# Instance normalisation of 32 x 576 planes: a compact gamma/beta load broadcast by TensorE, batched matmuls and merged stores

## Chip, cores, metric

One core of a Trainium2 chip. The metric is the device time of one execution in microseconds (us), median of several; lower is better. Ratios below are the mean time of one kernel's fast runs over that of the kernel before in the same rounds, so they are not quite the ratio of the medians quoted beside them. e1 to e4 ran on one chip, e5 to e8 on a second and e9 to e12 on a third; across chips only ratios are compared closely.

## The reference

```python
B, C, H, W = 32, 576, 16, 32        # x: bf16, g, b: bf16 of length C
mu = x.mean(axis=(-2, -1), keepdims=True)
var = ((x - mu) * (x - mu)).mean(axis=(-2, -1), keepdims=True)
xhat = (x - mu) / jnp.sqrt(var + 1e-5)
return xhat * g.reshape(1, -1, 1, 1) + b.reshape(1, -1, 1, 1)
```

18.87 MB are read and 18.87 MB written.

## The kernel before

All of x fits in SBUF. Each of the 128 partitions holds 144 consecutive planes ("tiles" 0 to 143: one plane of 512 elements per partition). Because 576 = 4 x 144, partition p needs row p mod 4 of gamma and beta seen as a 4 x 144 matrix. Tiles go in batches of two kinds: D takes its statistics on VectorE (`bn_stats`), P takes the mean by matmuls with a scaled identity and the variance by a ScalarE square with accumulation. ScalarE, GpSimd and, at the end, VectorE then apply scale and bias in place. A small scheduler in Python fixes every engine's order when the program is built.

```python
xr   = x.rearrange("b c h w -> (b c) (h w)").rearrange("(p n) f -> p n f", p=P)
g_src = bass.AP(g.tensor, 0, [[0, P // Q], [NT, Q], [1, NT]])     # 128 rows of 144, each row read 32 times
...
# GpSimd, behind its iota: gamma and beta by the software queue
em.eng.dma_start(g_sb[:], g_src).then_inc(sGB, 16)
em.eng.dma_start(b_sb[:], b_src).then_inc(sGB, 16)
...
# sync engine: 20 loads of 2, 2, 4, 8, 8, ... tiles, then one store for each batch or half batch
for ci, (a, e_) in enumerate(load_chunks):
    sp.dma_start(xt[:, a:e_, :], xr[:, a:e_, :]).then_inc(ld_sems[ci], 16)
for s_ in stores:
    dep_waits(em, [("ap", n) for n in range(s_["t0"], s_["t1"])])
    sp.dma_start(outr[:, s_["t0"]:s_["t1"], :], xt[:, s_["t0"]:s_["t1"], :]).then_inc(sST, 16)
...
# mean of a P tile: 8 matmuls of 64 columns, accumulated
for j in range(JB):
    ins = e.matmul(dst, ident[:], xt[:, n, j * NP_:(j + 1) * NP_], start=(j == 0), stop=(j == JB - 1), ...)
```

Of the kernel before, what the change touches and what calls it, by code (L numbers as in the profile page):

```python
# [11 lines left out]
F32 = mybir.dt.float32  # L12
BF16 = mybir.dt.bfloat16
I32 = mybir.dt.int32
# [5 lines left out]
    sq=704.0,  # L20
    mm=300.0,
    ap_A=705.0,
# [7 lines left out]
    lat=130.0,  # L30
    tile_dma=306.0,
    dma_start=1700.0,
    dma_fixed=60.0,
)
# [44 lines left out]

def build_plan(nt, pattern=None, load_chunks=None, cost=None, store_max=8, use_pool=True, use_pe=True):  # L80
    c = dict(COST)
# [34 lines left out]
    arrive = []  # L116
    t = c["dma_start"]
    for ci, (a, b_) in enumerate(load_chunks):
        t += (b_ - a) * c["tile_dma"] + c["dma_fixed"]
        arrive.append(t)  # L120
        for n in range(a, b_):
            tile_chunk[n] = ci

    tasks = {}
# [9 lines left out]
    add(("SQ0",), "A", 1400.0, [("DS",)], -1)  # L134
    add(("I0",), "G", 200.0, [], -1)
    add(("I1",), "V", 100.0, [("I0",)], -1)
    gb_arrive = 3000.0

# [7 lines left out]
    for b in batches:  # L146
        bi = b["idx"]
        w = b["t1"] - b["t0"]
        sm = c["small"] + c["small_per_elem"] * w
        if b["typ"] == "D":  # L150
            for n in range(b["t0"], b["t1"]):
                add(("bn", n), "V", c["bn"], [("ld", tile_chunk[n])], 10, bi)
            last_bn = [("bn", n) for n in range(b["t0"], b["t1"])]
            add(("R1", bi), "V", sm, last_bn, 1, bi)
            add(("R2a", bi), "V", sm, last_bn, 1, bi)
            add(("R2b", bi), "V", sm, last_bn, 1, bi)
            add(("T2", bi), "V", sm, [("R2a", bi), ("R2b", bi)], 1, bi)
            add(("V", bi), "V", sm, [("T2", bi), ("R1", bi)], 1, bi)
            add(("C1", bi), "A", c["sqrt"], [("V", bi)], 0, bi)
            ms_dep = ("R1", bi)  # L160
        else:
            for n in range(b["t0"], b["t1"]):
                deps = [("ld", tile_chunk[n]), ("I1",)]
                if b["pk"] >= psum_banks:
                    deps.append(("Rd", p_batches[b["pk"] - psum_banks]["idx"]))
                add(("mm", n), "T", c["mm"], deps, 10, bi)
            add(("Rd", bi), "V", c["rd_fixed"] + c["rd_per_tile"] * w, [("mm", n) for n in range(b["t0"], b["t1"])], 1, bi)
            add(("Cp", bi), "V", sm, [("Rd", bi)], 2, bi)
            for n in range(b["t0"], b["t1"]):
                deps = [("Rd", bi)]  # L170
                if len(sq_list) >= junk_n:
                    deps.append(("sq", sq_list[-junk_n]))
                tsq = add(("sq", n), "A", c["sq"], deps, 10, bi)
                tsq.idx_sq = len(sq_list)
                sq_list.append(n)
            add(("C1", bi), "A", c["sqrt"], [("sq", n) for n in range(b["t0"], b["t1"])], 0, bi)
            ms_dep = ("Cp", bi)
        add(("C2", bi), "V", sm + 25, [("C1", bi)], 0, bi)
        add(("C3", bi), "V", sm, [("C2", bi), ("gb",)], 0, bi)
        add(("C4", bi), "V", sm, [("C3", bi), ms_dep], 0, bi)  # L180
        add(("C5", bi), "V", sm, [("C4", bi), ("gb",)], 0, bi)
        for n in range(b["t0"], b["t1"]):
            add(("ap", n), None, None, [("C5", bi)], 50, bi)
# [3 lines left out]
    for ci in range(len(load_chunks)):  # L187
        done[("ld", ci)] = arrive[ci] - lat
    done[("gb",)] = gb_arrive - lat

# [33 lines left out]
    def pick(eng, t):  # L224
# [13 lines left out]
        if best is not None and best[1].cls <= 2:  # L238
            return best[1], None
        if eng == "G" and t < 1200.0 and not pending["G"]:  # L240
            return None, 1200.0
        if soon is not None and eng in ("V", "A"):
# [14 lines left out]
    while n_left > 0:  # L257
# [40 lines left out]
        tnow = min(cand)  # L298

    stores = []  # L300
    for b in batches:
        a = b["t0"]
        while a < b["t1"]:
            e = min(b["t1"], a + store_max)
            rdy = max(tasks[("ap", n)].end for n in range(a, e))
            stores.append(dict(t0=a, t1=e, ready=rdy))
            a = e
    stores.sort(key=lambda s: (s["ready"], s["t0"]))
    tq = arrive[-1]
    for s in stores:  # L310
        tq = max(tq, s["ready"] + 600.0) + (s["t1"] - s["t0"]) * c["tile_dma"] + c["dma_fixed"]
    makespan = max(tk.end for tk in tasks.values())
    return dict(
        nt=nt, batches=batches, load_chunks=load_chunks, stores=stores, tasks=tasks, streams=streams,
        tile_batch=tile_batch, tile_chunk=tile_chunk, makespan=makespan, est_total=tq + 2000.0,
        junk_n=junk_n, psum_banks=psum_banks, cost=c, use_pool=use_pool,
    )


def plan_summary(plan):  # L320
    lines = []
    st = plan["streams"]
    for e in ("V", "A", "G", "T"):
        busy = sum(t.dur for t in st[e])
        end = max([t.end for t in st[e]] or [0])
        kinds = {}
        for t in st[e]:
            kinds[t.key[0]] = kinds.get(t.key[0], 0) + 1
        lines.append(f"  {e}: n={len(st[e])} busy={busy/1e3:.1f}us end={end/1e3:.1f}us {kinds}")
    lines.append(f"  compute makespan {plan['makespan']/1e3:.1f}us  est total {plan['est_total']/1e3:.1f}us")  # L330
    return "\n".join(lines)

# [18 lines left out]
def bass_standalone__instancenorm__sampling_kernel(  # L351
# [29 lines left out]
    outr = out.rearrange("b c h w -> (b c) (h w)").rearrange("(p n) f -> p n f", p=P)  # L381
    g_src = bass.AP(g.tensor, 0, [[0, P // Q], [NT, Q], [1, NT]])
    b_src = bass.AP(b.tensor, 0, [[0, P // Q], [NT, Q], [1, NT]])

    with nc.Block() as block, contextlib.ExitStack() as es:  # L385
# [7 lines left out]
        junk = sb("junk", [P, junk_n, F], BF16)  # L393
        g_sb = sb("g_sb", [P, NT], BF16)
        b_sb = sb("b_sb", [P, NT], BF16)
        st = sb("st", [P, NT, 6], F32)
# [15 lines left out]
        d_ps = ps[:, 4, 2 * NT:3 * NT]  # L412
        rstd_ps = ps[:, 5, 0:NT]
        t_ps = ps[:, 5, NT:2 * NT]
        nm_ps = ps[:, 5, 2 * NT:3 * NT]

# [3 lines left out]
        def dep_waits(em, deps):  # L420
            need = {}
            for d in deps:
                if d[0] == "ld":
                    sem, val = ld_sems[d[1]], 16
                elif d[0] == "gb":
                    sem, val = sGB, 32
                else:
                    pt = tasks[d]
                    sem, val = sem_of[pt.eng], pt.idx + 1
# [15 lines left out]
        def emit_task(em, tk):  # L445
# [7 lines left out]
            elif k == "I0":  # L453
                ins = e.iota(iota_t[:], [[1, P]], base=0, channel_multiplier=-1)
            elif k == "SQ0":
                ins = e.activation(dummy[:, 1:2], dummy[:, 0:1], ACTF.Sqrt)  # L456
# [30 lines left out]
            elif k == "C2":  # L487
                t0, t1 = rng(tk.key[1])
                ins = e.reciprocal(rstd_ps[:, t0:t1], std_sb[:, t0:t1])  # L489
            elif k == "C3":  # L490
                t0, t1 = rng(tk.key[1])
                ins = e.tensor_tensor(scale_sb[:, t0:t1], g_sb[:, t0:t1], rstd_ps[:, t0:t1], ALU.mult)  # L492
            elif k == "C4":
                bb = batches[tk.key[1]]
                t0, t1 = bb["t0"], bb["t1"]
                if bb["typ"] == "D":
                    ins = e.scalar_tensor_tensor(t_ps[:, t0:t1], MA_ps[:, t0:t1, 0], -0.5, scale_sb[:, t0:t1], ALU.mult, ALU.mult)  # L497
                else:
                    ins = e.tensor_tensor(t_ps[:, t0:t1], nm_ps[:, t0:t1], scale_sb[:, t0:t1], ALU.mult)  # L499
            elif k == "C5":  # L500
                t0, t1 = rng(tk.key[1])
                ins = e.tensor_tensor(bias_sb[:, t0:t1], t_ps[:, t0:t1], b_sb[:, t0:t1], ALU.add)  # L502
            elif k == "sq":
# [4 lines left out]
            elif k == "mm":  # L508
                n = tk.key[1]
                bb = batches[tk.batch]  # L510
                slot = n - bb["t0"]
                dst = ps[:, bb["bank"], slot * NP_:(slot + 1) * NP_]
                ins = None
                for j in range(JB):
                    ins = e.matmul(dst, ident[:], xt[:, n, j * NP_:(j + 1) * NP_], start=(j == 0), stop=(j == JB - 1),  # L515
                                   skip_group_check=True)
# [14 lines left out]
        def run_stream(em, name):  # L531
            for tk in streams[name]:
                emit_task(em, tk)
                if name == "G" and tk.key[0] == "I0":
                    em.eng.dma_start(g_sb[:], g_src).then_inc(sGB, 16)
                    em.eng.dma_start(b_sb[:], b_src).then_inc(sGB, 16)

        @block.sync
        def _(sp):
            em = _Emit(sp, None, "SP")  # L540
            for ci, (a, e_) in enumerate(load_chunks):
                sp.dma_start(xt[:, a:e_, :], xr[:, a:e_, :]).then_inc(ld_sems[ci], 16)  # L542
            for s_ in stores:
# [49 lines left out]
```

## Time and profile before

| | before |
|---|---|
| median of the first 4 runs | 98.59 us (97.93 to 98.83) |
| span in the profile | 97.0 us |
| bytes over the span | 391 GB/s; 424 where the pipe is full |
| VectorE, ScalarE, GpSimd busy | 79%, 78%, 71% |
| stores | 24, of 2 to 8 tiles |
| matmuls | 400 of 64 columns |

Loads and stores run one after the other through one queue over sixteen DMA engines. The question for any change is what it does to that pipe: when it starts, when it has holes, and when the last of the sixteen engines finishes. The prediction shows the lines.

### The profile page before, as it was taken

To read this page: it belongs to the slowest core of one execution; us is meant where nothing else is said; L and a number is where in the kernel's file an instruction comes from. 1 tells how busy PE (TensorE), PEld (TensorE's weight loads), DVE (VectorE), ACT (ScalarE), POOL (GpSimd) and SP (SyncE) were. 2 spreads that over 40 slices of the span, in tenths; PEclk is the share of its full clock that TensorE was granted. 3 is DMA by queue.
4 is the path that set the end of the run, shared out by engine and by line. 5 is a ranking of instruction groups with operands and counts; after the bars stand their busy time and mean duration, and the time that the engine had idled before them with its cause. 6 is when DMAs were issued, how large, how long until landed. Compare 5 with 4: busy or idle time off the path is not lost.

```text
span 97.0 us, 1412 instructions
## 1 busy us (share of the span) xinstructions
PE 30.5 (31%) x400; PEld 27.6 (29%) x400; DVE 76.5 (79%) x244; ACT 75.3 (78%) x171; POOL 69.3 (71%) x97
## 2 busy tenths in 40 slices
PE   0220179259489189179767100000000000000000
PEld 0210169149388089079566000000000000000000
DVE  1532748899799899899799999999999999976000
ACT  6061627695599799999999999999999999996000
POOL 6000600498699599999999999999999996991000
DMA  1989999999999999999999999999999999999971
GB/s 40 298 205 379 429 432 422 432 422 399 419 426 426 429 422 405 412 432 422 420 405 409 431 429 430 425 423 411 422 432 429 429 414 438 421 411 426 423 290 58
DMA packets 6407, 37.91 MB, mean 391 GB/s; under 512 B 736, under 2 KB 736, under 8 KB 2944
## 3 DMA queue, kind: packets, MB, share of 16 engines
q1 hardware_dynamic: 6336, 37.75, 94.5%
q0 software_dynamic: 64, 0.07, 0.8%
q8 instruction: 3, 0.05, 0.2%
q14 instruction: 4, 0.03, 0.1%
HBM read 18.95 MB, written 18.87 MB: 390 GB/s over the span
## 4 chain that ended last, share of the span: by engine, by line
ACT 31%; DMA 29%; SPq 13%; DVE 10%; PE 5%; issue 2%; ACTq 1%
DMA xt<-in_x_dram 29%; ACT xt L520 20%; SPq L542 13%; ACT junk L506 11%; DVE st L459 8%; PE ps L515 5%; ACT std_sb L486 1%; ACTq L385 1%; DVE nm_sb L480 1%; DVE ps L489 0%; DVE ps L497 0%; DVE bias_sb L502 0%; DVE scale_sb L492 0%; DVE ps L462 0%; DVE ps L468 0%
## 5 line engine op out<-in xcount | busy, mean ns | idle before, releaser
L523 POOL TENSOR_SCALAR xt<-xt,scale_sb,bias_sb 128x512 bf16<-128x512 bf16 x90 | 67.6, 767 | 17.5 <-DVE bias_sb L502 8.8
L459 DVE BATCH_NORM_STATS2 st<-xt 128x6 f32<-128x512 bf16 x94 | 59.7, 678 | 5.4 <-DMA xt<-in_x_dram 5.4
L506 ACT ACTIVATE junk<-xt,nm_sb 128x512 bf16<-128x512 bf16 x50 | 35.4, 708 | 8.6 <-DVE nm_sb L480 8.6
L520 ACT ACTIVATE xt<-xt,bias_sb,scale_sb 128x512 bf16<-128x512 bf16 x50 | 36.6, 798 | 3.2 <-DVE bias_sb L502 3.2
L515 PE MATMUL ps<-xt,ident 128*128 128x64 bf16 x400 | 30.5, 276 | 23.2 <-DMA xt<-in_x_dram 23.0
L515 PEld LDWEIGHTS ps<-xt,ident 128*128 128x128 bf16 x400 | 27.6, 136 | 25.7 <-DMA xt<-in_x_dram 25.7
L506 ACT ACTIVATION_READ_ACCUMULATOR junk<-xt,nm_sb 128x1 f32 x50 | 9.4, 187 | 0.0
L480 DVE TENSOR_REDUCE nm_sb<-ps 128x8 f32<-128x512 f32 (+3 forms) x9 | 4.7, 525 | 4.3 <-PE ps L515 4.3
L486 ACT ACTIVATE std_sb<-v_sb 128x8 f32<-128x8 f32 (+6 forms) x19 | 3.7, 197 | 1.2 <-DVE v_sb L474 1.1
L489 DVE RECIPROCAL ps<-std_sb 128x8 f32<-128x8 f32 (+6 forms) x19 | 3.7, 198 | 0.8 <-ACT std_sb L486 0.7
L502 DVE TENSOR_TENSOR bias_sb<-ps,b_sb 128x8 f32<-128x8 f32 (+6 forms) x19 | 2.9, 158 | 0.2
L492 DVE TENSOR_TENSOR scale_sb<-g_sb,ps 128x8 f32<-128x8 bf16 (+6 forms) x19 | 2.8, 153 | 0.2
L523 DVE TENSOR_SCALAR xt<-xt,scale_sb,bias_sb 128x512 bf16<-128x512 bf16 x4 | 2.0, 553 | 0.0
L462 DVE TENSOR_REDUCE ps<-st 128x28 f32<-128x56 f32 (+4 forms) x10 | 1.9, 192 | 0.1
L456 ACT ACT_TABLE_LOAD x1 | 1.3, 1283 | 0.7 <-PEq L578 0.7
L497 DVE SCALAR_TENSOR_TENSOR ps<-ps,scale_sb 128x14 f32<-128x14 f32 (+4 forms) x10 | 1.7, 168 | 0.1
L468 DVE TENSOR_REDUCE ps<-st 128x14 f32<-128x28 f32 (+4 forms) x10 | 1.8, 177 | 0.0
L465 DVE TENSOR_REDUCE d_sb<-st 128x14 f32<-128x28 f32 (+4 forms) x10 | 1.7, 166 | 0.0
L471 DVE SCALAR_TENSOR_TENSOR q_sb<-d_sb,ps 128x14 f32<-128x14 f32 (+4 forms) x10 | 1.5, 154 | 0.0
L474 DVE TENSOR_TENSOR v_sb<-q_sb,ps 128x14 f32<-128x14 f32 (+4 forms) x10 | 1.5, 153 | 0.0
L483 DVE COPY ps<-nm_sb 128x8 f32<-128x8 f32 (+3 forms) x9 | 1.5, 162 | 0.0
L499 DVE TENSOR_TENSOR ps<-ps,scale_sb 128x8 f32<-128x8 f32 (+3 forms) x9 | 1.4, 159 | 0.1
(10 smaller groups left out, 2.4 us busy)
## 6 DMA issues: line engine op xcount, KB each, us to landing
xt<-in_x_dram SPq DMA_DIRECT2D x17, 1024.0 KB, 24.1
out_dram<-xt SPq DMA_DIRECT2D x10, 1024.0 KB, 10.3
out_dram<-xt SPq DMA_DIRECT2D x6, 768.0 KB, 8.2
out_dram<-xt SPq DMA_DIRECT2D x2, 640.0 KB, 14.4
out_dram<-xt SPq DMA_DIRECT2D x2, 512.0 KB, 14.4
out_dram<-xt SPq DMA_DIRECT2D x2, 384.0 KB, 14.1
xt<-in_x_dram SPq DMA_DIRECT2D x2, 256.0 KB, 2.9
xt<-in_x_dram SPq DMA_DIRECT2D x1, 512.0 KB, 7.5
```

The lines of the kernel that those rows point to most:

```text
L459: ins = e.bn_stats(st[:, n, :], xt[:, n, :])
L462: ins = e.tensor_reduce(MA_ps[:, t0:t1, :], st_pairs(t0, t1 - t0, 1, 2), AX.X, ALU.add)
L480: ins = e.tensor_reduce(nm_sb[:, t0:t1], src, AX.X, ALU.add)
L486: ins = e.activation(std_sb[:, t0:t1], v_sb[:, t0:t1], ACTF.Sqrt, bias=EPS, scale=1.0 / F)
L489: ins = e.reciprocal(rstd_ps[:, t0:t1], std_sb[:, t0:t1])
L492: ins = e.tensor_tensor(scale_sb[:, t0:t1], g_sb[:, t0:t1], rstd_ps[:, t0:t1], ALU.mult)
L502: ins = e.tensor_tensor(bias_sb[:, t0:t1], t_ps[:, t0:t1], b_sb[:, t0:t1], ALU.add)
L506: ins = e.activation(junk[:, j, :], xt[:, n, :], ACTF.Square, bias=nm_sb[:, n:n + 1], scale=1.0, accum_out=v_sb[:, n:n + 1])
L515: ins = e.matmul(dst, ident[:], xt[:, n, j * NP_:(j + 1) * NP_], start=(j == 0), stop=(j == JB - 1), skip_group_check=True)
L520: ins = e.activation(xt[:, n, :], xt[:, n, :], ACTF.Identity, bias=bias_sb[:, n:n + 1], scale=scale_sb[:, n:n + 1])
L523: ins = e.tensor_scalar(xt[:, n, :], xt[:, n, :], scale_sb[:, n:n + 1], bias_sb[:, n:n + 1], ALU.mult, ALU.add)
L542: sp.dma_start(xt[:, a:e_, :], xr[:, a:e_, :]).then_inc(ld_sems[ci], 16)
```

## The change

The intent is to take the 256 small pieces of the gamma/beta load off the DMA, to cut instructions on TensorE, and to write with fewer, larger stores.

```diff
-    g_src = bass.AP(g.tensor, 0, [[0, P // Q], [NT, Q], [1, NT]])
+    g_src = g.rearrange("(q n) -> q n", q=Q)                      # 4 rows of 144
...
+    elif k == "I1s":      # sel[q, p] = 1 where p mod 4 == q
+        ins = e.tensor_scalar(sel[:], iota_s[:], 0.0, None, ALU.is_equal)
+    elif k == "GB":       # broadcast to 128 partitions, in PSUM
+        e.matmul(g_ps, sel[:], gb4[:, 0, :], start=True, stop=True, ...)
+        ins = e.matmul(b_ps, sel[:], gb4[:, 1, :], start=True, stop=True, ...)
...
-                ins = e.matmul(dst, ident[:], xt[:, n, j * NP_:(j + 1) * NP_], ...)
+                ins = e.matmul(dst, ident[:], xt[:, t0:t1, j * NP_:(j + 1) * NP_], ...)   # a whole batch, up to 512 columns
...
-                    em.eng.dma_start(g_sb[:], g_src).then_inc(sGB, 16)      # GpSimd
-                    em.eng.dma_start(b_sb[:], b_src).then_inc(sGB, 16)
...
             for ci, (a, e_) in enumerate(load_chunks):
+                if ci == plan["gb_after"]:                                  # 2: between second and third load
+                    sp.dma_start(gb4[:, 0, :], g_src).then_inc(sGB, 16)
+                    sp.dma_start(gb4[:, 1, :], b_src).then_inc(sGB, 16)
                 sp.dma_start(xt[:, a:e_, :], xr[:, a:e_, :]).then_inc(ld_sems[ci], 16)
...
-    for b in batches:                                # one store per batch, at most 8 tiles
+    while a < nt:                                    # 16, 8 or 4 tiles in order of position, whatever the batch
```

1/std and the bias product move from PSUM to SBUF, since gamma and beta are now read from PSUM. The scheduler's constants change with it (cut).

## The prediction

> **What bounds the kernel now.** I read four things in turn: the page's utilisation slices and queue table, the windows view of the start and of the end, the waits of the engines, and the trace's completion records (each transfer leaves sixteen, one per DMA engine). First the page:
>
> ```profile
> PE 30.5 (31%) x400; PEld 27.6 (29%) x400; DVE 76.5 (79%) x244; ACT 75.3 (78%) x171; POOL 69.3 (71%) x97
> ...
> DMA  1989999999999999999999999999999999999971
> GB/s 40 298 205 379 429 432 422 432 422 399 419 426 426 429 422 405 412 432 422 420 405 409 431 429 430 425 423 411 422 432 429 429 414 438 421 411 426 423 290 58
> ...
> q1 hardware_dynamic: 6336, 37.75, 94.5%
> q0 software_dynamic: 64, 0.07, 0.8%
> q8 instruction: 3, 0.05, 0.2%
> ```
>
> No compute engine reaches 80%, but the sixteen DMA engines are full from the fourth slice to the thirty-eighth. Loads and stores share one queue (q1), so the kernel is one pipe: 37.75 MB at 424 GB/s is 89.0 us, and the span is 97.0. About 8 us is all that can be won without moving fewer bytes. It is lost at the two ends, which the windows view shows; its last two columns are the DMA's busy share and GB/s:
>
> ```profile
> 3.00:4.00 1.00, 0.00 (x0) 0.00 (x0) 0.47 (x1) 0.00 (x0) 0.00 (x0) 1.00 0.80 308
> 4.00:5.00 1.00, 0.82 (x13) 0.83 (x14) 0.96 (x5) 0.00 (x0) 0.00 (x0) 1.00 1.02 231
> 5.00:6.00 1.00, 0.43 (x7) 0.18 (x3) 0.68 (x7) 0.20 (x1) 0.00 (x0) 1.00 0.86 156
> 6.00:7.00 1.00, 0.00 (x0) 0.00 (x0) 0.02 (x1) 1.00 (x4) 0.00 (x0) 1.00 0.82 230
> 7.00:8.00 1.00, 0.00 (x0) 0.00 (x0) 0.00 (x0) 0.61 (x3) 0.00 (x0) 1.00 0.98 316
> ...
> 92.00:93.00 1.00, 0.00 (x0) 0.00 (x0) 0.00 (x0) 0.00 (x0) 0.00 (x0) 1.00 0.92 379
> 93.00:94.00 1.00, 0.00 (x0) 0.00 (x0) 0.00 (x0) 0.00 (x0) 0.00 (x0) 1.00 0.70 289
> 94.00:95.00 1.00, 0.00 (x0) 0.00 (x0) 0.00 (x0) 0.00 (x0) 0.00 (x0) 1.00 0.39 160
> 95.00:96.00 1.00, 0.00 (x0) 0.00 (x0) 0.00 (x0) 0.00 (x0) 0.00 (x0) 1.00 0.18 74
> ```
>
> From 4 to 8 us the DMA is as busy as ever but moves 231, 156, 230 and 316 GB/s: 0.93 MB where 1.70 was possible. That is 1.8 us lost, by a cause other than an empty queue. At the end the rate fades over 4 us instead of stopping: the engines do not finish together.
>
> The completion records join the two. The load of tiles 4 to 7 landed on its first engines at 5.2 us and on its last at 9.2; the last store landed at 94.2 to 96.6. An engine that fell behind at 5 us stays behind, because each moves the same sixteenth of every transfer (8 of its 128 rows), in order. Between 3.9 and 9.3 us run the 32 packets of the gamma and beta loads (2,304 bytes each, eight pieces of 288). They took 93 to 1,721 ns, 12.5 us together, and load packets beside them took up to 2,153 ns where an 8 KB packet takes 309. The two DMA-issue rows and the vector engine's wait show the consequence:
>
> ```profile
> xt<-in_x_dram SPq DMA_DIRECT2D x1, 512.0 KB, 7.5
> ...
> g_sb<-in_g_dram POOLq DMA_DIRECT2D x1, 36.0 KB, 5.9
> b_sb<-in_b_dram POOLq DMA_DIRECT2D x1, 36.0 KB, 7.5
> ```
> ```profile
> DVE st L459 <- DMA xt<-in_x_dram: 5.4, 2, 3.2
> DVE nm_sb L480 <- PE ps L515: 4.3, 7, 1.7
> ```
>
> The last column of the issue rows is us from issue to landing. 36 KB takes 5.9 and 7.5 us, and the 512 KB load beside it takes 7.5 against 2.9 for the 256 KB ones before it; VectorE waits 3.2 us for that load.
>
> **What the Trainium skill says.** "DMA: Bandwidth & Descriptors", section "Specifications", gives 512 B as the smallest transfer for line rate, with a read-modify-write below it. The trace agrees in direction: 2,304 bytes in 288-byte pieces took 93 ns at best and 389 on average; at the 8 KB rate they would take 87. Its section "Queues, rings and completion order" says that each engine takes turns between its queue rows at packet boundaries, so a slow small packet delays the loads on that engine; the slow load packets of 4 to 8 us agree. "TensorE: Matmul & The Clock Gate", section "Wait — 56ns, not 53.3ns?", gives N / 2.4 GHz + 2.5 ns from start to start: 216 ns for 512 columns. The trace has no such matmul; its 64-column ones, each with a 128-column weight load, take 4.87 us for 64, 76 ns each.
>
> **The change, part by part.**
>
> *Gamma and beta.* Removed: 256 pieces from 128 partitions by the software queue. Added: two loads of 4 rows of 288 bytes on q1, an iota, a mask and two matmuls of 144 columns. Their compute is off the path (first use is near 6 us). Gain on the fastest engine: its completions of the fourth load (8 tiles) came 3.6 us after those of the third (5.2 to 8.8), where 8-tile loads later come 2.5 us apart: 1.1 us. Gain from the spread: 2.4 us now between the first and last engine at the last store. I expect about 1.0 to remain, because the 8 KB and 16 KB instruction fetches (0.3 to 1.1 us each) still land on single engines: 1.4 us. Cost: the sync engine issues two more transfers (0.42 us each, as its other early issues) before the third load, whose issue moves from 1.64 to about 2.5 us. The first issue, at 0.74, had its first packet at 1.8, so third-load packets can come at 3.55; the first two loads complete at 3.5 to 4.1. So nearly no hole: I allow 0.2 us.
>
> *Stores.* 24 transfers of 2 to 8 tiles become 16: three of 16 tiles, eleven of 8, two of 4. An 8 KB packet takes 309 ns, 6 KB 234, 4 KB 159, 2 KB 84: about 9 ns per packet on top of the bytes. The sum over the store packets of one engine falls from 44.9 to 44.6 us: 0.35 us gained, on the path.
>
> *Matmuls.* 400 become 72, each up to 512 columns: an 8-tile batch goes from 4.87 us to an estimate of 8 x 216 = 1.7 us. PE is no bound, so this only shortens VectorE's 4.3 us of waits for PE and brings compute forward. 800 instructions become some 150, and the three 16 KB instruction fetches on q8 (about the size of 800 instructions at 64 bytes, an estimate) should mostly go. I have counted this in the smaller spread.
>
> Sum: 1.1 + 1.4 + 0.35 - 0.2 = 2.65 us. 98.59 - 2.65 = 95.9 us.
>
> **Does compute keep up?** It must, or the gain turns into a wait. Now the stores of tiles 112 to 119 are issued at 84.04, 131 to 136 at 88.31 and the last at 89.01. The pipe reaches each about 1.5 to 2.7 us after it could. In the new order 32 tiles (9.9 us) remain from tile 112 on; with the pipe's end near 92.5, that store's data should start at 82.6, so it must be issued by 81.5, which is 2.5 us earlier than now. VectorE is idle 9.4 us of the first 20 and only 3.1 of the next 69, so compute ends when the early idleness ends sooner. The third load landing 3 to 4 us earlier, and shorter PE waits, give 3 to 5 us. It should just do.
>
> **Rivals.** (1) *Compute becomes the bound:* only 1 to 2 us come forward, the in-order stores wait near tile 112, and the end is 96.8 to 97.5. For it: the thin margin and static order; against it: VectorE's idle time is mostly waiting for delayed loads and PE. (2) *The slow 4 to 8 us are the start-up of the load stream itself* (4 KB pieces, cold HBM), not gamma and beta: only the stores gain, 98.2. Against it: the rate had already reached 373 GB/s from 3.0 to 3.5 us and fell when the small packets began. (3) *The issue delay hurts:* if a four-row load costs 1 us to issue or blocks the queue, a hole of 1 us opens, 96.8. (4) *The spread disappears altogether* (few instruction fetches left): a further 1 us, 94.9.
>
> **Range and chances.** Rivals 1 and 3 at about 15% each and 4 at 20% lie on both sides of 95.9; rival 2 has 6%. I take 94.8 to 97.2. Faster by over 2% means under 96.6, which the central case and rival 4 give: 0.75. Within 2%: 0.24. Slower needs a hole of over 4 us: 0.01.
>
> **What would show it.** The q0 row gone; 4 to 8 us at 380 GB/s or more; the 512 KB load landing 3 to 4 us after issue, not 7.5; completions of the last store within about 1 us of each other; stores still issued ahead of the pipe, with DMA share near 1.0 through 80 to 90 us; 8-tile PE batches near 1.7 us. Wrong would be: a slow stretch at 4 to 8 us without the small packets (rival 2), DMA share dips after 60 us ended by an apply (rival 1), or a hole at 3 to 4 us (rival 3).

## The result

The changed kernel takes 96.27 us (median of 11 runs, 95.89 to 96.55); before, in the same rounds and the first runs, 98.74 (16 runs, 97.93 to 99.78). The ratio of the fast runs is 0.9762 (0.9728 to 0.9796): faster by 2.4%. The prediction of 95.9 us, 94.8 to 97.2, faster by over 2%, holds.

One thing in the times came up again in all later calls: the kernels with the gather on the software queue (before, e2, e3, e4) scatter (before: 97.91 to 100.95 us over 55 runs on one chip), while the changed kernel stays within 95.89 to 96.81 over all its 15 runs. e5, with the same gather on the sync queue, stays within 96.95 to 97.72. Runs over 1.5% above a kernel's fastest count as slow and are left out of the ratios, so these understate what a user of the old kernel would see.

The page of the changed kernel (the two rows of slices, then the queues, as the prediction showed them for before):

```profile
PE 23.1 (24%) x74; PEld 9.1 (10%) x74; DVE 77.2 (82%) x245; ACT 75.1 (79%) x171; POOL 68.4 (72%) x96
...
DMA  2799999999999999999999999999999999789995
GB/s 39 241 397 423 426 430 426 419 426 426 416 423 412 430 423 416 430 423 423 416 437 430 437 430 409 426 471 423 392 426 426 423 426 440 326 347 419 416 400 217
...
q1 hardware_dynamic: 5200, 37.75, 96.2%
q14 instruction: 5, 0.03, 0.1%
```

The q0 (gather) and q8 (instruction) rows are gone. The third slice moves 397 GB/s, before 205. New is a dip in slices 35 and 36. The windows of the changed kernel show both (last two columns: DMA share, GB/s):

```profile
3.00:4.00 1.00, 0.00 (x0) 0.00 (x0) 0.36 (x1) 0.00 (x0) 0.00 (x0) 1.00 0.84 244
4.00:5.00 1.00, 0.74 (x8) 0.75 (x8) 0.96 (x3) 0.00 (x0) 0.00 (x0) 1.00 0.63 197
5.00:6.00 1.00, 0.64 (x5) 0.15 (x3) 0.81 (x7) 0.35 (x1) 0.00 (x0) 1.00 1.01 406
6.00:7.00 1.00, 0.00 (x0) 0.00 (x0) 0.00 (x0) 1.00 (x4) 0.00 (x0) 1.00 1.01 397
7.00:8.00 1.00, 0.00 (x0) 0.00 (x0) 0.22 (x1) 0.47 (x3) 0.00 (x0) 1.00 1.00 414
...
82.00:84.00 2.00, 0.00 (x0) 0.00 (x0) 1.92 (x12) 2.00 (x5) 2.00 (x4) 0.50 0.57 238
...
93.00:94.00 1.00, 0.00 (x0) 0.00 (x0) 0.00 (x0) 0.00 (x0) 0.00 (x0) 0.50 0.45 180
```

From 5 us on the pipe is full, where before it crawled until 8. From 4 to 5 us it has a hole (share 0.63). From 82 to 84 it runs at 238 of 424 GB/s. The end is sharp: full until 93 us.

The issue row of the 512 KB load and VectorE's waits in the changed kernel answer to those of before (7.5 us to landing; 5.4 and 4.3 us of waiting):

```profile
xt<-in_x_dram SPq DMA_DIRECT2D x1, 512.0 KB, 5.4
```
```profile
DVE st L491 <- DMA xt<-in_x_dram: 3.8, 2, 1.9
DVE nm_sb L512 <- PE ps L547: 2.1, 3, 1.0
```

Where the time came from is read best from the completion records, first and last of the sixteen engines, in us from the span's start:

| | before | changed |
|---|---|---|
| third load issued | 1.64 | 2.37 |
| third load (512 KB) landed | 5.15 to 9.17 | 5.89 to 7.76 |
| fourth load landed | 8.76 to 11.67 | 8.35 to 10.29 |
| last load landed | 48.53 to 51.70 | 48.12 to 49.96 |
| store before that of tiles 112 to 119, landed | | 82.22 to 84.33 |
| store of tiles 112 to 119, issued | 84.04 | 82.50 |
| the same, landed | | 86.19 to 86.78 |
| last store landed | about 92.8 to 96.62 | 93.76 to 94.17 |

The 92.8 is an estimate. All stores count on one semaphore and a completion record does not name its engine, so records sorted by time mix two stores when the engines are further apart than one store takes; read that way the row would begin at 94.19, as the prediction had it. The packets tell more: the last store of before is 128 packets of 4 KB. The first began at 91.26, and eight of 155 ns, one engine's share, end at 92.5; the last ended at 96.28. So 3.8 us lie between the first and the last engine, not 2.4.

The slowest engine is 1.4 us earlier at the fourth load, 1.7 at the last load, 2.45 at the end. The slowest engine, not the mean, is what the end waits for.

### The profile page after: what moved, and what is told of

The parts are those of the page before. It is cut to its first block, busy times and chain, and to the rows that moved or that the text cites. A ratio compares the mean times of both kernels' runs of the same rounds, so it can differ in the third digit from the quotient of the medians.

```text
span 94.6 us, 749 instructions
## 1 busy us (share of the span) xinstructions
PE 23.1 (24%) x74; PEld 9.1 (10%) x74; DVE 77.2 (82%) x245; ACT 75.1 (79%) x171; POOL 68.4 (72%) x96
## 4 chain that ended last, share of the span: by engine, by line
ACT 53%; DMA 20%; SPq 6%; issue 5%; DVE 4%; PE 4%; DVEq 0%
ACT xt L552 29%; ACT junk L538 22%; DMA xt<-in_x_dram 20%; SPq L574 5%; PE ps L547 4%; DVE xt L555 2%; ACT std_sb L518 1%; DVE nm_sb L512 1%; DVE rstd_sb L521 0%; SPq L572 0%; DVE t_sb L529 0%; DVE scale_sb L524 0%; DVE bias_sb L534 0%; DVEq L407 0%; SPq L573 0%
## 5 line engine op out<-in xcount | busy, mean ns | idle before, releaser
L547 PE MATMUL ps<-xt,ident 128*128 128x512 bf16 (+3 forms) x72 | 22.7, 496 | 28.4 <-DMA xt<-in_x_dram 16.5
L547 PEld LDWEIGHTS ps<-xt,ident 128*128 128x128 bf16 x72 | 9.0, 139 | 41.8 <-issue 26.7
L521 DVE RECIPROCAL rstd_sb<-std_sb 128x8 f32<-128x8 f32 (+6 forms) x19 | 3.6, 194 | 2.1 <-ACT std_sb L518 2.1
L534 DVE TENSOR_TENSOR bias_sb<-ps,t_sb 128x8 f32<-128x8 f32 (+6 forms) x19 | 2.9, 157 | 0.2
L524 DVE TENSOR_TENSOR scale_sb<-ps,rstd_sb 128x8 f32<-128x8 f32 (+6 forms) x19 | 2.9, 155 | 0.2
L529 DVE SCALAR_TENSOR_TENSOR t_sb<-ps,scale_sb 128x14 f32<-128x14 f32 (+4 forms) x10 | 1.6, 162 | 0.2
L531 DVE TENSOR_TENSOR t_sb<-ps,scale_sb 128x8 f32<-128x8 f32 (+3 forms) x9 | 1.3, 147 | 0.1
```

Source lines behind the costliest of these rows:

```text
L521: ins = e.reciprocal(rstd_sb[:, t0:t1], std_sb[:, t0:t1])
L524: ins = e.tensor_tensor(scale_sb[:, t0:t1], g_ps[:, t0:t1], rstd_sb[:, t0:t1], ALU.mult)
L534: ins = e.tensor_tensor(bias_sb[:, t0:t1], b_ps[:, t0:t1], t_sb[:, t0:t1], ALU.add)
L547: ins = e.matmul(dst, ident[:], xt[:, t0:t1, j * NP_:(j + 1) * NP_], start=(j == 0), stop=(j == JB - 1), skip_group_check=True)
```

## The experiments

My theory A was that the 288-byte pieces slow single DMA engines from 4 to 9 us. Rival B: the slow stretch is start-up of the load stream itself. Rival C: the gain comes through compute (faster PE batches). Rival D: through larger stores. In e1 to e8 the scheduler was left to plan anew, as it does in the change; in e9 to e11 the order of all compute is that of the changed kernel. All twelve gave correct results.

### The three parts alone, and all but the first

**e1: gamma/beta alone.** The old matmul and store code put back into the changed kernel.

```diff
-        stores in order of position, 16/8/4 tiles; matmul over xt[:, t0:t1, ...]
+        stores per batch; matmul over xt[:, n, ...]
```

> Kernel before with only the gamma/beta part of the change (two 4-row loads on the sync queue, mask matmul); 64-column matmuls and 24 stores as before. Theory A (the 288-byte pieces slow single DMA engines between 4 and 9 us and they stay behind to the end): nearly the whole gain, 96.4 us, ratio about 0.978; the 512 KB load lands in about 5.4 us, completions of the last store within 1.5 us of each other. Rival B (the slow 4 to 8 us are start-up of the load stream): 98.3 us, 4 to 8 us still slow. Rival C (the faster PE batches bring the gain by bringing compute forward): no gain here beyond 0.5 us.

Measured: 96.85 us (96.75 to 97.15, 4 runs), ratio 0.9841 (0.9791 to 0.9891). The third load lands in 4.1 us on its last engine (issued at 2.35, landed at 6.45). Two thirds of the gain come from this part; C is out as the main cause. The spread at the last store is about 2.5 us by the packets, not 1.5: the three 16 KB instruction fetches of q8 are still there (1,018 to 1,071 ns each).

**e2: batched matmuls alone.**

> Kernel before with only the batched matmuls. Theory A: PE is no bound and compute is hidden behind the stores, so 98.5 us, within 0.4 us of before; VectorE's wait for PE falls from 4.3 to about 2 us and the instruction fetches of the q8 row go. Rival C (compute sets the time): 97.5 or less.

```diff
-    for n in range(t0, t1): 8 x matmul(..., xt[:, n, 64 columns])
+    8 x matmul(..., xt[:, t0:t1, 64 columns])
```

Measured: 98.72 us (median of the 10 fast runs of 20) beside 98.70 for before (28 fast of 55), ratio 1.001 (0.9972 to 1.0047). No gain alone. VectorE's wait for PE fell from 4.3 to 2.9 us, and q8 is gone.

**e3: merged stores alone.**

```diff
-    one store per batch, at most 8 tiles (24)
+    16, 8 or 4 tiles in order of position (16)
```

> Kernel before with only the merged stores. Theory A: 0.35 us from fewer packets, 98.3 us, unless the tail waits: in this order 32 tiles are left from tile 112 on, which compute delivers near 84 us, when the pipe is ready for it at about 84.5; then nothing is gained, 98.7. Rival D (larger stores are worth more, an overhead per transfer): 97.5 or less.

Measured: 98.84 us (11 fast runs of 20), ratio 1.0033 (0.9987 to 1.0079). No gain alone. D is out.

**e4: the changed kernel with the old gather on GpSimd.**

```diff
-    sp.dma_start(gb4[:, 0, :], g_src)       # 4 rows, sync; mask and matmul
+    pool.dma_start(g_sb[:], g_src)          # 128 rows, GpSimd
```

> Changed kernel with the gamma/beta part undone (128-row gather on the software queue), matmuls and stores as changed. Theory A: back to about 98.2 us, the slow stretch of 4 to 8 us returns and one or more engines are 2 us behind at the end. Rival B or C: 96.5, as the changed kernel.

Measured: 98.25 us (the 4 fast runs of 20, 97.2 to 98.61; all runs 97.2 to 99.89), ratio 0.994 (0.9882 to 0.9998). Most of the gain is lost, as A said (and as B said not, if taken as "nothing to do with this part"). The run profiled was a slow one, so I read only the times from it.

### What about the gather is slow? The pieces or the queue

**e5: the same 256 pieces, issued by the sync engine.** Kernel before, with the gather moved.

```diff
-    GpSimd: dma_start(g_sb[:], g_src); dma_start(b_sb[:], b_src)
+    sync, between second and third load: dma_start(g_sb[:], g_src); dma_start(b_sb[:], b_src)
```

> Kernel before, its 128-row gamma/beta gather unchanged in shape (256 pieces of 288 bytes) but issued by the sync engine on the load queue, after the second load. If the pieces themselves stall the DMA engines (small writes, 32 copies of the same bytes): as before, about 98.5 us or more, packets of 2,304 bytes at several hundred ns, 512 KB load landing near 7.5 us. If it is the software queue beside the load queue: as the gb-only kernel, 96.9 us, and the gather's packets near 93 ns each.

Measured: 97.20 us (96.95 to 97.72, 14 runs), ratio 0.987 (0.9837 to 0.9903). That is within 0.4 us of e1, on another chip, and the intervals of the ratios overlap. The windows of e5:

```profile
4.00:5.00 1.00, 0.73 (x14) 0.74 (x15) 0.97 (x3) 0.00 (x0) 0.00 (x0) 1.00 0.83 118
5.00:6.00 1.00, 0.30 (x6) 0.14 (x3) 0.82 (x7) 0.34 (x1) 0.00 (x0) 1.00 0.92 348
6.00:7.00 1.00, 0.00 (x0) 0.00 (x0) 0.00 (x0) 1.00 (x4) 0.00 (x0) 1.00 1.16 483
```

The pieces cost one bad second, in which most took 16 to 19 ns each, and then the pipe is full. So the small pieces as such, which my prediction blamed, cost at most a few tenths of a microsecond on this queue.

**e6: the compact load, issued by GpSimd.** The e1 kernel with only the issuing engine of gamma and beta changed; the third load is again issued at 1.64 us.

```diff
-    sync, between second and third load: dma_start(gb4[:, 0, :], g_src) ...
+    GpSimd, behind its two iotas:        dma_start(gb4[:, 0, :], g_src) ...
```

> Kernel before with the compact 4-row gamma/beta load and mask matmul, but issued by GpSimd on the software queue. If the pieces are the cause: 96.9 us or a little less, since the sync engine's third load is not delayed (96.3 to 96.9). If the software queue as such is: 98.5 us.

Measured: 97.51 us (97.14 to 98.54, 20 runs), ratio 0.9884 (0.9839 to 0.9929). Between the two expectations: the compact shape alone brings about 1.2 of the 1.6 per cent of e1 (0.9841), though the intervals overlap. But see its windows and its q0 row:

```profile
5.00:6.00 1.00, 0.24 (x5) 0.08 (x2) 0.78 (x7) 0.40 (x1) 0.00 (x0) 1.00 1.12 283
6.00:7.00 1.00, 0.00 (x0) 0.00 (x0) 0.00 (x0) 1.00 (x4) 0.00 (x0) 1.00 1.02 279
7.00:8.00 1.00, 0.00 (x0) 0.00 (x0) 0.18 (x1) 0.42 (x3) 0.00 (x0) 1.00 0.80 238
```
```profile
q0 software_dynamic: 64, 0.00, 0.0%
```

The slow stretch is back with eight pieces of 19 ns each in all. Load packets of 8 KB took up to 1,704 ns. Whatever slows them here, it is not the bytes or the count of the pieces. My next thought was the software queue as such.

### Matmuls and stores on top of the new load

**e7: the changed kernel with 64-column matmuls.**

```diff
-    8 x matmul(..., xt[:, t0:t1, 64 columns])
+    for n in range(t0, t1): 8 x matmul(..., xt[:, n, 64 columns])
```

> Changed kernel with the 64-column matmuls back. Theory A: PE speed is hidden, but the three 16 KB instruction fetches of the q8 row come back and each puts one DMA engine about 0.9 us behind: 96.6 us, 0.3 over the changed kernel (96.3). Rival C (compute pace sets the tail, the store of tiles 112 to 119 is issued later): 97 or more, with DMA share under 1 between 82 and 87 us. If the gb-only kernel's lost 0.6 us is all due to the stores: 96.3.

**e8: the changed kernel with the 24 stores of before.**

```diff
-    16, 8 or 4 tiles in order of position (16)
+    one store per batch, at most 8 tiles (24)
```

> Changed kernel with the 24 per-batch stores back. Theory A: the 0.35 us of packets return, 96.6 us; no dip of the DMA share at 82 to 87 us, since only 24 tiles are left from tile 112 on in that order. If the changed kernel's end is set by its wait for tiles 112 to 119: 96.0 or less.

Measured: e7 96.48 us (3 fast runs, 96.37 to 96.82, ratio 0.9841; a fourth, 97.86, was slow), e8 96.56 us (4 runs, 96.52 to 96.73, ratio 0.9844). The changed kernel itself was 96.27 and, on another chip, 96.50. Both are where A put them, but they lie no further from these two medians than 0.3 us, and the two differ by 0.2: the times do not resolve the two parts singly. Together they are the step from e1 (0.9841) to the changed kernel (0.9762), some 0.4 to 0.6 us by the medians, which come from different chips. The window of e8 answers whether the dip at 82 us costs anything:

```profile
82.00:84.00 2.00, 0.00 (x0) 0.00 (x0) 1.46 (x11) 2.00 (x6) 2.00 (x4) 0.50 0.99 410
```

Without the dip (0.99 against 0.57) the last store lands at 94.36 us; with it, at 94.17. The dip is paid by engines that would otherwise have waited at the end: in the changed kernel the engines that were ahead idle there (the first had finished the store before at 82.22), while the slowest finishes it at 84.33 and the next at 86.78, 2.45 us later, which is simply the time of 8 tiles (eight 8 KB packets of 309 ns on each engine). e8 alone would not prove that the dip is free, since its smaller stores cost packets too; the 84.33 does, because the data of the next store, issued at 82.50, could begin at about 83.7 (an estimate: its first completion, 86.19, less 2.45).

### The queue, the moment, or the start of the stream

**e9: compact load on ScalarE's hardware queue.** A second hardware queue, at the very start, so that the sync engine need not issue gamma and beta.

```diff
-    sync, between second and third load: dma_start(gb4[:, 0, :], g_src) ...
+    ScalarE, first of all:               dma_start(gb4[:, 0, :], g_src) ...
```

> Changed kernel, compute order unchanged, with the two compact gamma/beta loads issued by ScalarE's hardware queue ahead of its table load, so that the sync engine issues the third load at 1.65 us instead of 2.37. If the 0.6 GB/s share and 200 GB/s or less at 4 to 5 us are an issue hole: that second is at 300 GB/s or more and all later completions come about 0.7 us earlier; the time falls only by some 0.2 to 0.4 us (95.9 to 96.1), since the store of tiles 112 to 119 then waits for compute. If the slow 4 KB packets of 3.6 to 5 us are start-up of the load stream (rival B in small): unchanged, 96.3.

(The "0.6 GB/s share" in it should read: the DMA share of 0.6.)

Measured: 97.42 us (96.90 to 98.10), ratio 0.9879 (0.9796 to 0.9962), beside 96.50 for the changed kernel on the same chip. I had expected a gain of 0.2 to 0.4 us and got a loss of 0.9. The windows of e9 and its row of the new queue:

```profile
4.00:5.00 1.00, 0.82 (x8) 0.77 (x8) 0.97 (x4) 0.00 (x0) 0.00 (x0) 1.00 0.88 279
5.00:6.00 1.00, 0.56 (x5) 0.12 (x2) 0.72 (x7) 0.42 (x1) 0.00 (x0) 1.00 0.96 270
6.00:7.00 1.00, 0.00 (x0) 0.00 (x0) 0.00 (x0) 1.00 (x4) 0.00 (x0) 1.00 1.00 311
7.00:8.00 1.00, 0.00 (x0) 0.00 (x0) 0.02 (x1) 0.39 (x3) 0.00 (x0) 1.00 0.88 283
```
```profile
q10 hardware_dynamic: 16, 0.00, 0.0%
```

The hole at 4 to 5 us is smaller, as it should be with the third load issued at 1.64, but now the stretch to 8 us is slow. And all eight pieces of gamma and beta had started by 2.96 us and taken 16 to 19 ns each; the last completion came at 3.46. When 8 KB packets took up to 1,922 ns at 5 to 8 us, nothing of gamma and beta was in the DMA any more, and the queue was no software queue.

The slow stretch does not account for the whole 0.9 us, though. At the fourth load the sixteen engines of e9 are 0.6 us later than in the changed kernel on average (9.40 against 8.78), but the slowest is only 0.1 later (10.43 against 10.29), and 0.2 at the last load (50.16 against 49.95). The other 0.7 us of the slowest engine came during the stores before tile 112 (landed at 85.21 against 84.33). What cost it there was not found.

**e10: e9 with merged stores for tiles 0 to 59 only.** An attempt at a version that beats both.

```diff
-    16, 8 or 4 tiles in order of position for all tiles
+    [0,16) [16,32) [32,46) [46,60), then one store per batch, at most 8 tiles
```

> As e9, with merged stores only for tiles 0 to 59 and per-batch stores after that, so that 24 instead of 32 tiles are left when tiles 112 to 119 are needed. If the changed kernel's end is set by that wait and by the slowest DMA engine together: no dip of the DMA share between 82 and 87 us, and 95.6 us (0.7 less than changed). If the end is bandwidth and packets alone: 96.3.

Measured: 97.70 us (97.09 to 98.02), ratio 0.9886. No dip at the tail (share 1.03 from 84 to 88 us) and no gain: the last store lands on its slowest engine at 95.67, some 3 us after the first by the packets, and again the slowest engine sets the end. No version beats the changed kernel.

**e11: an unused software-queue load in mid-stream.** The compact load once more, into a spare tile, in the changed kernel.

```diff
+    GpSimd, behind its 14th apply: dma_start(spare[:, 0, :], g_src); dma_start(spare[:, 1, :], b_src)
```

> Changed kernel plus two unused 4-row loads of gamma and beta (8 pieces of 288 bytes in all) issued by GpSimd on the software queue after its 14th apply, near 24 us, in the middle of the load stream. If the software queue as such slows the load packets (as e6 showed at 5 to 10 us): load packets of 400 to 1700 ns for some 4 us after it, 1 us or more added: 97.0 to 97.5. If it harms only the start of the stream: 96.3, as the changed kernel.

Measured: 96.44 us (96.31 to 96.53), ratio 0.9774, beside 96.50 for the changed kernel. Its pieces passed at 27.7 to 28.6 us. The windows around:

```profile
26.00:28.00 2.00, 0.78 (x2) 0.28 (x3) 2.00 (x4) 2.00 (x7) 2.00 (x3) 0.58 1.03 427
28.00:30.00 2.00, 2.00 (x6) 0.73 (x5) 1.91 (x5) 1.53 (x5) 0.79 (x2) 0.50 1.00 410
```

Nothing. A small software load as such harms nothing while the stream is in full run. With e9, where the stretch came without a software queue, my thought after e6 falls as well.

**e12: the changed kernel again,** unedited, for the chip of e9 to e11.

> The changed kernel itself on the same chip as e9 to e11, for comparison: 96.3 us, within 0.3 of its first runs under any theory.

Measured: 96.50 us (96.07 to 96.81), ratio 0.9778 (0.9721 to 0.9836).

### What the runs say together

| gamma/beta load | third load issued | GB/s at 5-6, 6-7, 7-8 us | ratio |
|---|---|---|---|
| before: gather, GpSimd | 1.64 | 156, 230, 316 | 1 |
| e6: compact, GpSimd | 1.64 | 283, 279, 238 | 0.9884 |
| e9: compact, ScalarE | 1.64 | 270, 311, 283 | 0.9879 |
| e5: gather, sync | 2.97 | 348, 483, 393 | 0.9870 |
| e1: compact, sync | 2.35 | 447, 393, 401 | 0.9841 |
| changed: compact, sync | 2.37 | 406, 397, 414 | 0.9762 |

Two things separate. First, the gather on the software queue does harm of its own: from before to e6 the issue time of the loads stays and the time falls by 1.2% (its 32 packets took 12.5 us in the profile of before, e6's pieces 0.2 us). Second, the slow stretch of the loads does not need it: it is there in the three kernels of the table that issue the third load at 1.64 us, whatever carries gamma and beta, and gone after 5 us in all that issue the two small transfers from the sync engine first, which puts the third load off by 0.7 us or more. All fourteen profiles (that of e4 is of a slow run) divide so: 156 to 344 GB/s in each microsecond from 5 to 8 in the first kind (before, e2, e3, e4, e6, e9, e10), 348 to 483 in the second. In e9 no gamma/beta packet is left when it happens. That fits rival B, start-up of the load stream, with one addition that I had not thought of: something that the change puts between the second and third load removes it. Whether that is the pause of 0.7 us, or the small transfers in the same queue, was not separated: that wants the kernel before with nothing but a wait of 0.7 us ahead of its third load. Why the stream stumbles without it stays open too, and e9 leaves open how much of the 2.4% the stretch is worth.

A third thing stands in the completion records and was overlooked at first: what the three 16 KB instruction fetches of q8 do. In e1 a fetch of 1.06 us starts at 20.35 us; before it the last engine lands each load 1.07 us after the first, from the next load on 2.15. Between their landings of the fourth and of the last load the first engine takes 39.7 to 40.0 us in every kernel. The last takes 40.9 to 41.2 in e1, e3, e5, e6 and e7, which have the fetches, and 39.7 to 40.4 in the kernels without. So the fetches put the slowest engine about a microsecond behind in those kernels, and the batched matmuls, with which they go (e2, e8), help at least by that. Before is the exception: it has the fetches, and its last engine takes 40.0.

## Why the prediction was right, and where it was not

**The bound.** Right. A full pipe, lost time at both ends, and the slowest of the sixteen engines at the end: every run is read by that. e2 and e3 gain nothing, and in both the start is as slow as before (217 to 284 GB/s from 5 to 8 us).

**The cause of the slow 4 to 8 us.** This step failed in part. The prediction put it to the 288-byte pieces and gave rival B 6%. e5 (same pieces, no slow stretch past 5 us) and e9 (no pieces left, slow stretch) show that the pieces neither make it by themselves nor are needed for it. That removing them was worth 2% is, as far as shown, right for another reason, and so partly by luck: the change also took them off the software queue (e6 against before) and, by the way, put a pause and two small transfers ahead of the third load (e9 against the changed kernel, where it is 0.1 to 0.6 us at the fourth load). My argument against B was that 373 GB/s had been reached before the pieces began: a coincidence in time, taken for a cause. It was not even a coincidence: the rate had fallen to 277 GB/s at 3.4 to 3.6 us and 266 at 3.6 to 3.8, and the first packet of the pieces starts at 3.83.

**The terms of the sum.** Fastest engine, 1.1 us: the step from third to fourth load shrank from 3.61 to 2.46 us, 1.15, as predicted. Cost of the later issue, allowed at 0.2: the third load's first completion came 0.74 us later (5.15 to 5.89). That term was mis-sized, and rival 3 had the better number. But e9 shows that this cost cannot be saved in the obvious way. Spread, 1.4: at the last load it fell from 3.17 to 1.84 us, by 1.33. The size is near the prediction's, but not by its numbers: it had 2.4 falling to 1.0, and the 2.4 was misread (3.8 by the packets); only the wait near tile 112 let the engines close up to 0.4. So the predicted sum for the load part, 2.3 us, was 1.74 at the slowest engine's last load (0.41 on the first engine, 1.33 of spread).

The other 0.71 us came after that, where I had 0.35 for the packets of the stores. That sum was wrong too: with 611 ns for a 16 KB packet, measured in the changed kernel, the store packets of one engine add up to 44.4 us and not 44.6, which makes the term 0.5. The runs agree without resolving it: from last load to last store the slowest engine took 44.4 to 45.0 us in kernels with 24 stores and 43.9 to 45.0 in those with 16. Total 2.45 at the slowest engine, 2.65 predicted: a cost too small by 0.5 and a last part too small by 0.4 nearly cancelled, which is luck.

**Matmuls.** The term failed: an 8-tile batch took 3.57 us, not 1.7. The timeline of TensorE in the changed kernel, and in before:

```profile
20.32 3.57 PE L547 MATMUL ps<-xt,ident 128*128 128x512 bf16 x8 [5.23 <-DMA xt<-in_x_dram]
```
```profile
34.39 4.87 PE L515 MATMUL ps<-xt,ident 128*128 128x64 bf16 x64 [2.53 <-DMA xt<-in_x_dram]
```

3.57 us for 8 is 446 ns for 512 columns, and from the start of one to the start of the next it is 427. That is the figure that the page "TensorE: Matmul & The Clock Gate", section "Wait — 56ns, not 53.3ns?", gives for the cold clock (427), not that for the warm one (216), which I took. Its section "What's actually happening" has the clock low after some 3.4 us without work, and TensorE stands idle 3.8 to 5.2 us before these batches, so I should have chosen the other figure. The clock column of the windows seems to speak against it: it has 1.00 from 20 to 40 us of the changed kernel, where three of these batches lie. But the first clock record of that trace is at 43.27 us, and where there is none the column prints 1.00. In e9 the records begin earlier, with full clock from 39.49 to 46.31 us, and the batch that falls there runs at 216 ns from start to start:

```profile
40.30 1.90 PE L609 MATMUL ps<-xt,ident 128*128 128x512 bf16 x8 [1.36 <-DMA xt<-in_x_dram]
```

e8 and e10 show the same; in e11 the record is at half clock from 26.32 to 43.39 us, and the batch at 39.65 takes 3.59 us. So the clock is the reason, and both figures of the page agree with these traces. With 64-column matmuls an 8-tile batch took 3.54 to 3.60 us in e7, no more than the wide ones at the low clock; why it takes 4.87 in before is open.

**Compute keeps up.** "It should just do" failed by a microsecond: the store of tiles 112 to 119 was issued 1.5 us earlier (84.04 to 82.50), where 2.5 were needed and 3 to 5 hoped for. The third load landed 1.4 us earlier (9.17 to 7.76), not the 3 to 4 that this step counted on; the matmuls may be part of it too, which was not tested. Rival 1's dip is there. It cost nothing, since the slowest engine was still busy (e8). The range held because a new wait fell into slack that my sum had counted as removed; that was luck, not foresight.

## What to carry to other kernels

When sixteen DMA engines carry a stream, read the first and the last of each load's sixteen completion records: the 2.9 us that lay between them at 10 us were still there at the end of before, and a wait that lets the others idle is free until it reaches the slowest. Before blaming small transfers for a slow stretch that they coincide with, move them in time or to another queue and see whether it follows; here the stretch stayed when they had gone, and went when the same transfers were put into the load queue. A part that gains nothing alone can still count once another is mended: with the old start the batched matmuls gained nothing (e2); with the new one, the three instruction fetches that they take away stood out as a microsecond on the slowest engine (e1 has them).

## What the Trainium skill lacked or had wrong

- "DMA: Bandwidth & Descriptors", section "Specifications", has transfers under 512 B as below line rate. On the sync engine's queue most 288-byte pieces took 16 to 19 ns (e5; 288 bytes at the 8 KB packets' rate would be 11), and the kernel with 256 of them was at most some 0.4 us slower than that with 8 (e5 97.20, e1 96.85, on two chips). On the software queue the same 256 took 12.5 us in packets of eight. The page does not set the queues apart in this.
- The same page, section "Issuing engines are not separate DMA queues", says that issuing from several engines "will only save the time on the sequencer". Here, moving two 1.1 KB loads from the sync engine to ScalarE saved that time (third load at 1.64 instead of 2.37 us) and yet the kernel was 0.9 us slower (e9 97.42, e12 96.50; why is open). No page tells of a slow stretch at the start of a load stream (156 to 316 GB/s for 3 us, where 400 to 450 follow) that is gone where two small transfers and 0.7 us come ahead of the third load.
- I found on no page that an early delay of some DMA engines lasts to the end of a kernel: before, 2.9 us lie between the first and the last engine at the fourth load (near 10 us), 3.2 at the last load and 3.8 at the last store (by its packets), with equal shares of work.
